# Relu and square of the boundary units: one VectorE instruction in place of two on ScalarE

## The chip, the cores and the metric

The program runs on one core of one Trainium2 chip. A core has five engines that work through their own instruction queues in order: TensorE (PE in the profile, with the weight loads apart as PEld), VectorE (DVE), ScalarE (ACT), GpSimd (POOL) and SyncE (SP, which only issues transfers here). They signal each other by semaphores. The metric is the device time of the whole program in microseconds (us).

## The reference

```
p_packed = sm_attn(p, k, v)                       # 32 packed rows per batch and head
out      = sm_attn(q, p_packed, p_packed)         # 8 batches x 576 tokens, 8 heads x 64
x = out as (4608 tokens, 512)
h = maximum(x @ w_in, 0);  x = (h * h) @ w_out    # 512 -> 2048 -> 512
logits = x @ w_gate + modality_bias[modality_id]  # 8 experts, the greatest is taken
out[tokens of e] = gate * (maximum(x @ w1[e], 0) @ w2[e])   # 512 -> 1024 -> 512
```

All inputs are float32. A float32 product is made on TensorE as three products of a high and a low part (hi x hi, hi x lo, lo x hi), and making those parts is most of the work of VectorE and ScalarE.

## The kernel before, in words

The 4608 tokens go through the middle layers in 12 **units** of 384 tokens (`UT` = 3 tiles of 128). For unit `u` the first layer is done in 16 **blocks** `f` of 128 hidden columns (`layer1`), each followed, one block later, by the second layer of the block before (`layer2`, 9 matmuls of 512 columns into the accumulators `acc`, L534). The packed values of a batch are multiplied with `w_in` ahead of time, so `layer1` multiplies attention weights (`a2T`) with a block that belongs to one batch (`ring`, `head`).

A batch has 576 tokens, so every third unit (1, 4, 7 and 10) holds tokens of two batches. The other eight units make a block by 12 matmuls (L508), and ScalarE reads the sum from PSUM for relu (L523, `r<-ph`). A **boundary unit** makes each of its two **halves** of 192 tokens by four matmuls (L514, L516 twice, L517) into two groups of columns of one bank; ScalarE copies one group to `r` (L520) and VectorE adds the other (L521). Then relu (L523, `r<-r`), square (L524) and the high part (L525, writes `ghl`) follow on ScalarE, and the low part (L527, `ghl<-r,ghl`) on VectorE. There are two buffers each of `r` and `ghl` and two PSUM banks `h`.

Beside this each unit carries background work, paced by counters in the loop over `f`: the attention of the next unit (`att2`), splitting the next batch's blocks (L426 on ScalarE, L427 on GpSimd), and, for the unit before, the copy of the accumulators to `rows` (`evacuate`, L545 on VectorE) and 24 multiplications with the gate's weights, one for each tile and expert (`tail`, L555). In units 4 and 10 `route` follows: it ranks the tokens by expert, with one-hot rows (`od`, `om`, L689 and L691), matmuls of them (`pl`, L699) and two additions to the list `lst` (L705). In unit 10 `tables` makes from `lst` the row numbers `idx_g` (L745), by which GpSimd gathers the rows of the first group of the expert layers (`xg`, L790); TensorE turns these (`tr`, L804), and the expert layers follow.

The order of instructions on each engine in this part is set by the framework's scheduler: it takes ready instructions by priority, and L520 to L527 stand 40 places ahead of their place in the program (`high_priority(offset=CHAIN)`). Once written, an engine's order is fixed.

Of the kernel before, what the change touches and what calls it, by code (L numbers as in the profile page):

```python
# [15 lines left out]
AF = mybir.ActivationFunctionType  # L16
ALU = mybir.AluOpType
# [9 lines left out]
def tile_pack_attention_moe_moe2(  # L27
# [15 lines left out]
    nc = tc.nc  # L43
# [211 lines left out]
    def bank(tag, name):  # L255
        if "early" in held:
            return held["early"].tile([P, 512], F32, tag="e", name=name, bufs=4)
        return held["ps" + tag].tile([P, 512], F32, tag=tag, name=name)
# [148 lines left out]
    def block(b, f):  # L407
        return (NF * b + f) % RING

    def blocks(i, n):  # L410
        t = held["head" if i < HEAD else "ring"]
        i -= 0 if i < HEAD else HEAD
        return t[:, i : i + n]
# [16 lines left out]
    def parts(t0, n):  # L430
        got, t = [], t0
        while t < t0 + n:
            b = t // S
            e = min(t0 + n, (b + 1) * S)
            got.append((b, t - t0, e - t))
            t = e
        return got
# [59 lines left out]
    def layer1(u, f):  # L497
        a = a2T[u]
        r = held["g"].tile([P, UW], F32, tag="r", name="r")
        hl = held["g"].tile([P, 2, UW], F32R, tag="ghl", name="ghl")  # L500
        ps = parts(u * UW, UW)
        if len(ps) == 1:
            ph = bank("h", "ph")[:, :UW]
            t = blocks(block(ps[0][0], f), 1)[:, 0]
            i = 0
            for c in range(NPC):
                for x, y in ((0, 0), (0, 1), (1, 0)):
                    nc.tensor.matmul(ph, t[:, x, c, :], a[:, y, c, :], start=(i == 0), stop=(i == 3 * NPC - 1))  # L508
                    i += 1
        for b, off, n in ps if len(ps) > 1 else ():  # L510
            ph = bank("h", "ph")[:, : 2 * n]
            both = ph.rearrange("p (y n) -> p y n", y=2)
            t = blocks(block(b, f), 1)[:, 0]
            nc.tensor.matmul(both, t[:, 0, 0, :], a[:, :, 0, off : off + n], start=True, stop=False)  # L514
            for c in range(NPC):
                nc.tensor.matmul(both[:, 0], t[:, 1, c, :], a[:, 0, c, off : off + n], start=False, stop=False)  # L516
            nc.tensor.matmul(both, t[:, 0, 1, :], a[:, :, 1, off : off + n], start=False, stop=True)  # L517
            with tc.high_priority(offset=CHAIN):
                rn = r[:, off : off + n]
                nc.scalar.activation(out=rn, in_=both[:, 1], func=AF.Copy)  # L520
                nc.vector.tensor_tensor(out=rn, in0=both[:, 0], in1=rn, op=ALU.add)  # L521
        with tc.high_priority(offset=CHAIN if u else 0):
            nc.scalar.activation(out=r, in_=ph if len(ps) == 1 else r, func=AF.Relu)  # L523
            nc.scalar.activation(out=r, in_=r, func=AF.Square)  # L524
            nc.scalar.activation(out=hl[:, 0], in_=r, func=AF.Copy)  # L525
            eng = nc.vector if u else nc.gpsimd
            eng.tensor_tensor(out=hl[:, 1], in0=r, in1=hl[:, 0].bitcast(F32), op=ALU.subtract)  # L527
        return hl
# [399 lines left out]
    with tc.manual_schedule():  # L928
# [90 lines left out]
        for f in range(NF):  # L1019
            if f:  # L1020
                load_out(f + 3)
            hl = layer1(0, f)
            pw_next("tt")
            if f > 3:
                pw_next("th")
            if f > 2:
                next(bg, None)
            put()
            if pend is not None:
                if f == 1:  # L1030
                    held["acc"] = [bank("acc", "acc") for _ in range(UT)]
                layer2(held["acc"], *pend)
            pend = (f, hl)
            if f:
                halve_out(f)
            if f == 0:
                compact(NQ - 1)
            if 0 < f < NU - 1:
                for _ in conv_out(f + 1):
                    pass  # L1040
            if f in (4, 7):
                for _ in conv_in(14 + f // 7):
                    pass
            if f + 2 < NF:
                split_pw(0, f + 2)
            ahead(0, 0, f)
# [29 lines left out]
    for u in range(1, NUN):  # L1076
        pair, k = divmod(u, UPP)
        last = u == NUN - 1
        if u == 1:
            st1.close()  # L1080
            nc.sync.dma_start(
                wgb.rearrange("p e d -> p (e d)"), w_gateT.rearrange("e d -> (e d)").partition_broadcast(P)
            )
            held["xg"] = ctx.enter_context(tc.tile_pool(name="xg", bufs=2, side="right"))
        bga = Paced([] if last else [att2(u + 1)], R_ATT)
        for f in range(NF):
            hl = layer1(u, f)
            if pend is not None:
                second_layer()
            pend = (u, f, hl)  # L1090
            if f == 0:
                gens, n = background(u)
                bgt = Paced(gens, n / ((NF - 6 if last else NF) - 1.5))
            bga.step()
            bgt.step()
            ahead(pair, k, f)
            if last and f == NF - 6:
                bgt.finish()
                bgt = Paced([weights1(0)], 1)
        bga.finish()  # L1100
        bgt.finish()
# [80 lines left out]
```

## Time and profile before

| | before |
|---|---|
| median of 3 runs | 1226.17 us (1223.72 to 1228.62) |
| the profiled execution's own time | 1226.34 us |
| its span, first to last instruction | 1224.5 us |
| PE busy | 1186.8 us (97%) |
| DVE busy | 810.2 us (66%) |
| ACT busy | 625.6 us (51%) |
| POOL busy | 278.0 us (23%) |

Busy times count an instruction from its start to its end. On DVE and ACT the next instruction may start before the end of the last one, so a row of back-to-back instructions advances by less than the sum of their lengths.

### The profile page before, as it was taken

The numbers are of one execution on the slowest core, as the hardware profiler recorded it, in microseconds if no ns is written. First come the engines' busy times: TensorE is split into PE (matmuls) and PEld (weight loads), VectorE is DVE, ScalarE is ACT, GpSimd is POOL, SyncE is SP. The second block draws the span as 40 slices with busy tenths as digits, with TensorE's granted clock in tenths as the row PEclk, the third lists the DMA queues.
The fourth block names the chain that finished last, engine by engine and source line by source line (L and its number), as shares of the span: only waits on it lengthen the run. The fifth ranks groups of instructions, "written<-read, shape, count | busy, mean of one in ns | idle before, by whom it ended". The sixth has DMA issues, their size and how long they took to land.

```text
span 1224.5 us, 17896 instructions
## 1 busy us (share of the span) xinstructions
PE 1186.8 (97%) x6036; PEld 976.1 (80%) x6036; DVE 810.2 (66%) x2123; ACT 625.6 (51%) x1332; POOL 278.0 (23%) x347
## 2 busy tenths in 40 slices
PE   6999999999999999999999999999999999999995
PEld 4776568888888888888888887888888888888884
DVE  4777989597669857695975797889445345345331
ACT  5667777755467664567554676524233333333220
POOL 2316563221022320032210222003112122123001
PEclk9999999999999999999999999999999999999998
DMA  9999883220112220122101113307254254254211
GB/s 327 365 335 312 268 268 103 87 72 27 44 44 80 61 70 9 48 67 87 61 27 44 44 68 100 130 7 245 80 180 156 75 185 156 69 191 151 71 56 37
DMA packets 76086, 147.13 MB, mean 120 GB/s; under 512 B 7504, under 2 KB 27088, under 8 KB 75856
## 3 DMA queue, kind: packets, MB, share of 16 engines
q1 hardware_dynamic: 70224, 126.72, 31.3%
q0 software_dynamic: 5760, 19.17, 4.8%
q8 instruction: 49, 0.80, 0.3%
q14 instruction: 53, 0.43, 0.1%
HBM read 109.92 MB, written 33.85 MB: 117 GB/s over the span
## 4 chain that ended last, share of the span: by engine, by line
PE 76%; DMA 11%; DVE 8%; issue 2%; ACT 1%; POOL 1%; SPq 1%; POOLq 0%; DVEq 0%; ACTq 0%
PE acc L534 26%; PE h L828 17%; PE o L855 16%; PE ph L508 10%; DMA early<-in_v 4%; DVE rows L555 3%; DMA pw_d<-pws 2%; PE s L456 2%; PE tr L804 1%; PE ph L516 1%; PE ph L517 1%; PE ph L514 1%; DMA wgb<-in_k 1%; DVE r L521 1%; DMA rows<-in_k 1%
## 5 line engine op out<-in xcount | busy, mean ns | idle before, releaser
L534 PE MATMUL acc<-wb,ghl 128*128 128x512 f32 x1728 | 442.5, 399 | 1.9 <-ACT ghl L525 1.6
L534 PEld LDWEIGHTS acc<-wb,ghl 128*128 128x128 f32 x1728 | 317.9, 189 | 68.8 <-ACT ghl L525 6.4
L555 DVE SCALAR_TENSOR_TENSOR rows<-rows,wgb 128x512 f32<-128x512 f32 x288 | 212.1, 736 | 4.5 <-DMA wgb<-in_moe_w_gate 0.9
L828 PE MATMUL h<-xt,wb 128*128 128x512 f32 x864 | 213.1, 397 | 0.0
L828 PEld LDWEIGHTS h<-xt,wb 128*128 128x128 f32 x864 | 161.7, 188 | 38.5
L527 DVE TENSOR_TENSOR ghl<-r,ghl 128x384 fp32r<-128x384 f32 x176 | 106.8, 608 | 77.0 <-ACT ghl L525 76.9
L525 ACT ACTIVATE ghl<-r 128x384 fp32r<-128x384 f32 x192 | 100.0, 522 | 81.6 <-PE acc L534 79.2
L840 DVE SCALAR_TENSOR_TENSOR ht<-h,ht 128x512 fp32r<-128x512 f32 x72 | 49.3, 688 | 114.1 <-ACT ht L840 114.1
L840 ACT ACTIVATE ht<-h 128x512 fp32r<-128x512 f32 x72 | 42.7, 592 | 144.2 <-PE h L828 141.1
L866 POOL DMA_INDIRECT out<-wgb,idx_s x36 | 37.4, 1040 | 336.1 <-DVE wgb L864 251.4
L855 PE MATMUL o<-head,ht 128*128 128x512 f32 x432 | 111.8, 395 | 0.2 <-DVE wgb L864 0.2
L855 PE MATMUL o<-ring,ht 128*128 128x512 f32 x432 | 111.8, 395 | 0.0
L524 ACT ACTIVATE r<-r 128x384 f32<-128x384 f32 x192 | 99.9, 523 | 4.4
L855 PEld LDWEIGHTS o<-head,ht 128*128 128x128 f32 x432 | 80.4, 188 | 18.6 <-DVE wgb L864 0.6
L855 PEld LDWEIGHTS o<-ring,ht 128*128 128x128 f32 x432 | 80.4, 188 | 16.7
L427 POOL TENSOR_TENSOR ring<-praw,ring 128x256 fp32r<-128x256 f32 x70 | 58.8, 840 | 153.4 <-ACT ring L426 125.3
L523 ACT ACTIVATE r<-ph 128x384 f32<-128x384 f32 x128 | 62.0, 485 | 61.6 <-PE ph L508 33.8
L508 PE MATMUL ph<-a2T,ring 128*128 128x384 f32 x420 | 85.1, 339 | 0.0
L508 PEld LDWEIGHTS ph<-a2T,ring 128*128 128x128 f32 x420 | 74.7, 188 | 4.6
L508 PE MATMUL ph<-a2T,head 128*128 128x384 f32 x348 | 72.1, 341 | 1.1 <-ACT head L426 0.9
L761 DVE TENSOR_TENSOR wb<-wraw,wb 128x1024 fp32r<-128x1024 f32 x36 | 44.0, 1224 | 43.4 <-ACT wb L760 42.8
L427 POOL TENSOR_TENSOR head<-praw,head 128x256 fp32r<-128x256 f32 x50 | 43.2, 864 | 113.2 <-ACT head L426 113.0
(208 smaller groups left out, 1649.4 us busy)
## 6 DMA issues: line engine op xcount, KB each, us to landing
wraw<-in_moe_w SPq DMA_DIRECT2D x72, 512.0 KB, 3.5
praw<-pw_d SPq DMA_DIRECT2D x112, 128.0 KB, 2.6
x_d<-rows SPq DMA_DIRECT2D x12, 792.0 KB, 3.8
qT<-in_q SPq DMA_DIRECT2D x36, 256.0 KB, 2.9
early<-in_v SPq DMA_DIRECT2D x16, 512.0 KB, 7.8
pw_d<-pws SPq DMA_DIRECT2D x16, 512.0 KB, 5.9
stage<-in_moe_w_in SPq DMA_DIRECT2D x14, 512.0 KB, 9.1
pw_d<-pws SPq DMA_DIRECT2D x16, 384.0 KB, 4.7
```

The costliest lines, as they stand in the source:

```text
L427: nc.gpsimd.tensor_tensor(out=t[:, 1], in0=raw, in1=t[:, 0].bitcast(F32), op=ALU.subtract)
L508: nc.tensor.matmul(ph, t[:, x, c, :], a[:, y, c, :], start=(i == 0), stop=(i == 3 * NPC - 1))
L523: nc.scalar.activation(out=r, in_=ph if len(ps) == 1 else r, func=AF.Relu)
L524: nc.scalar.activation(out=r, in_=r, func=AF.Square)
L525: nc.scalar.activation(out=hl[:, 0], in_=r, func=AF.Copy)
L527: eng.tensor_tensor(out=hl[:, 1], in0=r, in1=hl[:, 0].bitcast(F32), op=ALU.subtract)
L534: nc.tensor.matmul(acc[t], hl[:, x, t * P : (t + 1) * P], w_out_block(f)[:, y, :], start=(f == 0 and x == 0 and y == 0), stop=(f == NF - 1 ...
L555: nc.vector.scalar_tensor_tensor(out=junk, in0=row[:, t, :DM], scalar=1.0, in1=wgb[:, e], op0=ALU.mult, op1=ALU.mult, accum_out=one)
L761: nc.vector.tensor_tensor(out=t[:, 1, :], in0=raw, in1=t[:, 0, :].bitcast(F32), op=ALU.subtract)
L828: nc.tensor.matmul(ph, half1(g, c)[:, x, f * P : (f + 1) * P], xs[c][:, y, :], start=(i == 0), stop=(i == 3 * NDC - 1),)
L840: done = nc.scalar.activation(out=h[:, 0, :], in_=ph, func=AF.Relu), nc.vector.scalar_tensor_tensor(out=h[:, 1, :], in0=ph, scalar=0.0, in ...
L855: nc.tensor.matmul(po, hs[f][:, x, t * P : (t + 1) * P], second(f)[:, y, :], start=(i == 0), stop=(i == 3 * NFE - 1),)
```

## The change: what it does

In a boundary unit the two ScalarE instructions L523 and L524 are replaced by one VectorE instruction that computes max(r, 0) * r, from `r` and `r` in SBUF, in place. There are 4 x 16 such blocks: 64 relu and 64 square instructions of 128x384 leave ScalarE and 64 SCALAR_TENSOR_TENSOR of 128x384 come to VectorE. The other units are as they were.

```diff
         with tc.high_priority(offset=CHAIN if u else 0):
-            nc.scalar.activation(out=r, in_=ph if len(ps) == 1 else r, func=AF.Relu)
-            nc.scalar.activation(out=r, in_=r, func=AF.Square)
+            if len(ps) == 1:
+                nc.scalar.activation(out=r, in_=ph, func=AF.Relu)
+                nc.scalar.activation(out=r, in_=r, func=AF.Square)
+            else:
+                nc.vector.scalar_tensor_tensor(out=r, in0=r, scalar=0.0, in1=r, op0=ALU.max, op1=ALU.mult)
             nc.scalar.activation(out=hl[:, 0], in_=r, func=AF.Copy)
             eng = nc.vector if u else nc.gpsimd
             eng.tensor_tensor(out=hl[:, 1], in0=r, in1=hl[:, 0].bitcast(F32), op=ALU.subtract)
```

The changed file is three lines longer: the new instruction is L527 there, and the old L525, L527, L534, L545, L555, L699, L705 and L804 are L528, L530, L537, L548, L558, L702, L708 and L807.

The scheduler also writes another order. This is VectorE in the middle of unit 10, among the logit multiplications; `r<-ph,r` is the addition of a half, `ghl<-r,ghl` the low part of a block. Before:

```order
L555 SCALAR_TENSOR_TENSOR rows,lg_all<-rows,wgb 128x512 x3
L527 TENSOR_TENSOR ghl<-r,ghl 128x384
L521 TENSOR_TENSOR r<-ph,r 128x192
L555 SCALAR_TENSOR_TENSOR rows,lg_all<-rows,wgb 128x512
L521 TENSOR_TENSOR r<-ph,r 128x192
L555 SCALAR_TENSOR_TENSOR rows,lg_all<-rows,wgb 128x512 x3
L527 TENSOR_TENSOR ghl<-r,ghl 128x384
```

The changed kernel at the same place:

```order
L530 TENSOR_TENSOR ghl<-r,ghl 128x384
L521 TENSOR_TENSOR r<-ph,r 128x192
L558 SCALAR_TENSOR_TENSOR rows,lg_all<-rows,wgb 128x512
L527 SCALAR_TENSOR_TENSOR r<-r 128x384
L558 SCALAR_TENSOR_TENSOR rows,lg_all<-rows,wgb 128x512
L521 TENSOR_TENSOR r<-ph,r 128x192
L530 TENSOR_TENSOR ghl<-r,ghl 128x384
```

A block now has one instruction more on VectorE, and fewer logit multiplications stand between two low parts.

The second place is TensorE at the end of unit 10, from the matmuls of the routing (`pl`) to the first turned rows of the gather (`tr`). Before:

```order
L699 MATMUL pl<-od,om 128x184
L534 MATMUL acc<-wb_1710,ghl 128x512 x3
L514 MATMUL ph<-a2T,head 128x384
L516 MATMUL ph<-a2T,head 128x192 x2
L517 MATMUL ph<-a2T,head 128x384
L514 MATMUL ph<-a2T,head 128x384
L516 MATMUL ph<-a2T,head 128x192 x2
L517 MATMUL ph<-a2T,head 128x384
L534 MATMUL acc<-wb_1710,ghl 128x512 x9
L514 MATMUL ph<-a2T,head 128x384
L516 MATMUL ph<-a2T,head 128x192 x2
L517 MATMUL ph<-a2T,head 128x384
```

After these rows stand, before, one `tr` matmul, nine more of `acc`, five `tr`, and six more of `acc`. In the changed kernel:

```order
L702 MATMUL pl<-od,om 128x184
L537 MATMUL acc<-wb_1802,ghl 128x512 x12
L807 MATMUL tr<-ident,xg 128x128 x3
L487 MATMUL ta_7664<-ident,e 128x128 x2
L807 MATMUL tr<-ident,xg 128x128 x5
L508 MATMUL ph<-a2T,head 128x384 x2
```

The last `pl` moved behind all the first-layer matmuls of unit 10, and 12 matmuls of `acc` are left between it and the first `tr`.

The third place is VectorE just behind that, where `idx_g` is made in the changed kernel:

```order
L708 TENSOR_TENSOR lst<-pl,lst 128x92
L527 SCALAR_TENSOR_TENSOR r<-r 128x384
L469 TENSOR_TENSOR e<-s_7531,mx 128x256
L708 TENSOR_TENSOR lst<-pl,lst 128x92
L745 TENSOR_SCALAR s_7559<-lst 128x28
L749 SCALAR_TENSOR_TENSOR s_7560<-lst,slot 128x28
L530 TENSOR_TENSOR ghl<-r,ghl 128x384
L748 CAST idx_g<-s_7559 128x28
```

Here a relu-and-square has come in between the two additions to `lst`, and a low part stands ahead of `idx_g`.

Counted in the two orders, VectorE holds from the copy of the accumulators that opens a unit's logits to the 24th logit multiplication (the **front** of the unit):

| front of unit | halves L521 | new instruction | low parts | logits | others |
|---|---|---|---|---|---|
| 1, before / after | 16 / 20 | 0 / 9 | 9 / 9 | 24 / 24 | 20 / 23 |
| 4, before / after | 16 / 18 | 0 / 8 | 8 / 8 | 24 / 24 | 12 / 12 |
| 7, before / after | 15 / 18 | 0 / 9 | 6 / 8 | 24 / 24 | 21 / 22 |
| 10, before / after | 14 / 16 | 0 / 8 | 7 / 7 | 24 / 24 | 6 / 6 |
| 10, to the second addition to `lst` | 26 / 30 | 0 / 15 | 13 / 14 | 24 / 24 | 82 / 82 |

## Rows read from the trace of the kernel before

**Rows 1.** Windows: start:end, length, busy time (instructions) of each engine, clock, DMA
```profile
core 0: us, PE busy (x) PEld busy (x) DVE busy (x) ACT busy (x) POOL busy (x), PEclk, DMA share, GB/s
184.40:221.00 36.60, 36.09 (x203) 30.98 (x202) 34.90 (x104) 25.54 (x66) 11.30 (x14) 1.00 0.33 98
350.90:381.00 30.10, 29.54 (x160) 25.46 (x160) 29.85 (x86) 21.85 (x55) 9.34 (x10) 1.00 0.20 59
381.00:402.00 21.00, 21.00 (x128) 17.86 (x127) 19.76 (x88) 15.11 (x38) 4.74 (x7) 1.00 0.28 95
516.80:547.00 30.20, 28.87 (x163) 24.80 (x162) 30.08 (x90) 20.08 (x54) 10.35 (x12) 1.00 0.22 65
547.00:571.20 24.20, 24.20 (x136) 21.33 (x136) 14.24 (x41) 17.39 (x44) 7.72 (x11) 1.00 0.31 99
684.40:713.70 29.30, 28.11 (x147) 23.85 (x146) 28.91 (x92) 20.60 (x53) 7.73 (x9) 1.00 0.13 37
713.70:735.00 21.30, 21.30 (x125) 18.32 (x124) 19.22 (x90) 15.02 (x37) 5.32 (x6) 1.00 0.27 101
```

**Rows 2.** Timeline of TensorE in unit 4: start, length, operation, [idle before, releaser]
```profile
352.54 2.26 PE L534 MATMUL acc<-wb,ghl 128*128 128x512 f32 x9
...
355.78 2.25 PE L534 MATMUL acc<-wb,ghl 128*128 128x512 f32 x9
...
375.88 0.44 PE L514 MATMUL ph<-a2T,head 128*128 128x384 f32 x1 [0.30 <-DVE r L521]
...
377.55 0.73 PE L534 MATMUL acc<-wb,ghl 128*128 128x512 f32 x2 [0.26 <-ACT ghl L525]
```

**Rows 3.** Groups by line and shape: busy, mean ns of one, idle before
```profile
L555 DVE SCALAR_TENSOR_TENSOR rows<-rows,wgb 128x512 f32<-128x512 f32 x288 | 212.1, 736 | 4.5 <-DMA wgb<-in_moe_w_gate 0.9
...
L527 DVE TENSOR_TENSOR ghl<-r,ghl 128x384 fp32r<-128x384 f32 x176 | 106.8, 608 | 77.0 <-ACT ghl L525 76.9
...
L524 ACT ACTIVATE r<-r 128x384 f32<-128x384 f32 x192 | 99.9, 523 | 4.4
...
L523 ACT ACTIVATE r<-r 128x384 f32<-128x384 f32 x64 | 33.3, 521 | 17.8 <-DVE r L521 17.7
```

**Rows 4.** Timeline of VectorE in unit 4
```profile
370.61 0.56 DVE L527 TENSOR_TENSOR ghl<-r,ghl 128x384 fp32r<-128x384 f32 x1
371.08 0.35 DVE L521 TENSOR_TENSOR r<-ph,r 128x192 f32<-128x192 f32 x1
...
372.24 0.35 DVE L521 TENSOR_TENSOR r<-ph,r 128x192 f32<-128x192 f32 x1
372.51 0.68 DVE L555 SCALAR_TENSOR_TENSOR rows<-rows,wgb 128x512 f32<-128x512 f32 x1
373.12 0.07 DVE L555 DVE_READ_ACCUMULATOR rows<-rows,wgb 128x1 f32 x1
```

**Rows 5.** Line 527: ns of one, least/median/greatest, first and last start
```profile
L527 DVE TENSOR_TENSOR ghl<-r,ghl x176: 501/557/1093, 185.1 to 793.8; 128x384 fp32r<-128x384 f32 x176
```

**Rows 6.** Timeline of VectorE at the start of unit 10's logits
```profile
684.48 0.69 DVE L545 COPY rows<-acc 128x512 f32<-128x512 f32 x1 [1.36 <-PE acc L534]
```

**Rows 7.** Chain that ended last, end of unit 10: start, time on the chain, what
```profile
730.84 0.27 DVE lst L705
...
736.27 5.70 DMA xg<-x_d,idx_g
...
742.02 0.44 PE tr L804 x2
```

**Rows 8.** Timeline of TensorE from the last `pl` to the `tr` matmuls
```profile
730.11 0.41 PE L699 MATMUL pl<-od,om 128*128 128x184 f16 x3
...
735.74 0.33 PE L804 MATMUL tr<-ident,xg 128*128 128x128 f32 x1 [0.68 <-DMA xg<-x_d,idx_g]
...
738.63 0.33 PE L804 MATMUL tr<-ident,xg 128*128 128x128 f32 x1 [0.36 <-DMA xg<-x_d,idx_g]
...
742.02 0.44 PE L804 MATMUL tr<-ident,xg 128*128 128x128 f32 x2 [1.12 <-DMA xg<-x_d,idx_g]
```

## The prediction

> **What bounds the kernel now.** I read the windows first, cut at the boundary units: from where VectorE copies the accumulators until the logits are through, and the rest of the unit [rows 1]. In the fronts of units 4, 7 and 10 TensorE is busy 29.54 of 30.10 us, 28.87 of 30.20 and 28.11 of 29.30, and VectorE 29.85, 30.08 and 28.91. Both are full, so the bound there is whichever falls behind. ScalarE is busy some 70% (21.85 of 30.10). In unit 1 VectorE has 1.7 us left in 36.6. In the second parts the picture splits: in unit 7 VectorE is busy 14.24 of 24.20, but in units 4 and 10, where the routing stands, 19.76 of 21.00 and 19.22 of 21.30.
>
> The timeline of TensorE in unit 4 says who is behind. A block takes 355.78 - 352.54 = 3.24 us while all goes well; near the end of the front the first layer waits for a half's addition on VectorE and then the second layer for the high part [rows 2]. The high part was late because its chain began late, at an addition that stood behind logit multiplications in VectorE's queue. So in the fronts VectorE sets the pace, by a little: TensorE's idle time in the four windows is 0.51 + 0.56 + 1.33 + 1.19 = 3.6 us.
>
> The chain that ended last shows one more place [rows 7]. At the end of unit 10 it runs from VectorE's second addition to `lst` (done at 730.84 + 0.27 = 731.11), through `idx_g` and four gathers on GpSimd, to the last rows landing and the `tr` matmuls at 742.02: 10.9 us that nothing shortens. TensorE waits three times in it, 0.68, 0.36 and 1.12 us [rows 8], although most of it was covered by matmuls of unit 10. From there the expert layers start, so a microsecond later in `lst` is one later at the end, as long as the cover doesn't grow.
>
> **What the change removes.** In each of the 64 blocks ScalarE loses 521 + 523 ns [rows 3], 67 us in all. ScalarE is not the bound in any of these windows, so this time itself is worth nothing. What may be worth something is that the way from the second half's addition to the high part gets shorter. I set that to nothing, since it was the wait in VectorE's queue ahead of that way which held TensorE; the limit on the gain is the 3.6 us of idle time, taken up as a rival below.
>
> **What it adds, and its price.** The trace has no relu-and-square on VectorE. The nearest row is the low part, L527: two inputs in SBUF, the same 384 elements. Back to back it advances the queue by 371.08 - 370.61 = 0.47 us [rows 4]; its median of 557 ns is longer since the next instruction starts some 0.08 us before its end, and its mean is 608 [rows 3, 5], which with the same overlap gives 0.53. I take 0.50. Bounds: 0.42 (the least length, 501 ns, less the overlap) and 0.61, the advance of a logit multiplication (373.12 - 372.51), which is the same operation with 512 elements. A half's addition advances the queue by 372.51 - 372.24 = 0.27.
>
> The Trainium skill ("Perfetto Trace Analysis", Optimizing Scalar/DVE Operations) advises moving work from VectorE to ScalarE where VectorE is saturated; this change goes the other way. If all 64 new instructions counted in full, as that rule read strictly would have it, the sum would be 64 x 0.50 = 32 us slower; by the windows only part of them fall where VectorE is full, and I count those alone.
>
> **Unit by unit.** The changed order spreads the 24 logit multiplications over more blocks, so the front holds more work, but TensorE also gets more done in it. For each front: the added VectorE work less 3.24 us for each block (two halves) that TensorE does more.
>
> Unit 4: eight new instructions and two additions, 8 x 0.50 + 2 x 0.27 = 4.5, less one block: 1.3 us. Unit 7: 9 x 0.50 + 3 x 0.27 + 2 low parts x 0.47 = 6.25, less one and a half blocks, 4.86: 1.4 us. Unit 1: 9 x 0.50 + 4 x 0.27 = 5.6 (with three small ones some 6), less two blocks, 6.5: nothing. Behind the fronts unit 1 and unit 7 have VectorE time to spare (10 us in unit 7 [rows 1]), which covers the rest of the new instructions; were that cover gone, the seven left in unit 7 would cost 3.5. In unit 4 the rest of the routing can run into unit 5, where nothing gathers by it.
>
> Unit 10 is where the list must be ready. From the copy at 684.48 [rows 6] to the end of the second addition at 731.11 VectorE needs 46.6 us, and it is busy for all but some 2 of them [rows 1]. The changed order holds 15 new instructions, four half additions and one low part more up to the same point: 15 x 0.50 + 4 x 0.27 + 0.47 = 9.1 us. The matmuls of the last `pl` have moved behind all first-layer matmuls of the unit, and 12 matmuls of `acc` (12 x 2.25 / 9 = 3.0 us by [rows 2]) are left as cover for the 10.9 us, where 27 of `acc` and three halves were. What was cover now lies ahead of `pl`, so when the rows land TensorE has done about the same work as before, and the expert layers start later by the whole 9.1. Queued behind the `tr` matmuls on TensorE is all of unit 11, which can't step in.
>
> The sum is 0 + 1.3 + 1.4 + 9.1 = 11.8 us on the profiled execution's 1226.34, 1238.1; the median of the runs is 0.2 lower, so I say 1238. With 32 new instructions in the sum (8, 9 and 15), the price bounds shift it by -2.6 and +3.5; if unit 10 fills its idle 2 us, by -2. That gives 1233.5 to 1241.6 for this case.
>
> **Rivals.** First, the list is not the bound: the changed order asks VectorE for the routing later, because TensorE's work before it is longer, and the 10.9 us stay covered. Then unit 10 costs only its front, 8 x 0.50 + 2 x 0.27 - 3.24 = 1.3, and the whole is 1226.3 + 4.0 = 1230.3. For it speaks that TensorE, too, comes later to `pl` in the new order; against it that VectorE had about 2 us idle where 9 are added, and that less cover, not more, stands behind `pl`. It needs 7.8 of the 9.1 hidden.
>
> Second, on the other side: TensorE's waits in the fronts come from the length of the way over ScalarE, not from VectorE's queue. The way gets shorter by 521 + 523 less some 500 ns in each block, and the idle 3.6 us go: 1226.3 - 3.6 = 1222.7. For it speaks that one of the two waits in rows 2 is for ScalarE's high part; against it VectorE's 98 to 99%. It decides if the front of unit 4 gets shorter than 30.1 us for the same blocks.
>
> Third, worse: the new instruction meets GpSimd. The low part's longest is 1093 ns against a median of 557 [rows 5], and most of GpSimd's busy time, 9.34 us in the front of unit 4 [rows 1], is tensor work on SBUF. If half of the 32 are lengthened by 0.53 us, 8.5 us come on top: 1246.6. The Trainium skill ("SBUF — State Buffer", Who interferes with whom) says that a VectorE instruction with two inputs in SBUF and a GpSimd instruction that reads SBUF exclude each other, the later one waiting to the end. By that rule the trace agrees, since the longest is the median and one GpSimd instruction's remainder; my 0.53 in the price holds the usual share of such cases already.
>
> That the change does nothing can't be: the order shows 64 instructions moved.
>
> **How the numbers follow.** Less than 0.5% (6.1 us) is about what a measurement of this kernel can't tell from no change: 1220.0 to 1232.3. The forecast gets 0.57, the first rival 0.20, the second 0.10, the third 0.13. Slower by over 0.5% are the forecast and the third, with a little of the first: 0.72. The second lies within 0.5% in the main, with a tail past 1220 where the waits' restarts go as well: faster 0.05. The rest, 0.23, is the same. The range leaves out most of the second rival and the upper half of the third: 1226 to 1244; the forecast's own is 1233.5 to 1241.6.
>
> **What would show it.** In the trace of the changed kernel: 64 instructions of 128x384 on VectorE's new line with a median near 0.56 us; VectorE at 98% or more in the fronts of units 4, 7 and 10; from the copy that opens unit 10's logits to the second `lst` addition some 56 us in place of 46.6; TensorE's waits for the gather and for `pl` together some 10 us in place of 2.2 (the 9.1 less the front's 1.3, added to them). Units 2, 5 and 8 should be as long as before. The prediction is wrong if the new instruction runs well under 0.42 or over 0.61 us, if `lst` is late but TensorE's waits before `tr` don't grow, or if the way over ScalarE was what counted and the fronts shrink.

## The result, and the profile after

The changed kernel takes 1241.1 us, the median of six runs (1238.97 to 1244.12), beside 1226.22 us for the kernel before on the same chip (six runs). The ratio is 1.0136, with a 95% interval of 1.0116 to 1.0155: the change makes the kernel slower. The prediction said 1238 with a range of 1226 to 1244.

The profiled execution of the changed kernel took 1239.04 us, its span is 1237.2 us. The first part of its page gives busy time, share of the span and instructions of each engine:

```profile
PE 1194.5 (97%) x6036; PEld 978.1 (79%) x6036; DVE 842.1 (68%) x2187; ACT 562.9 (45%) x1204; POOL 276.9 (22%) x347
```

VectorE rose by 31.9 us to 842.1, ScalarE fell by 62.7 to 562.9. The time went up by about half of what VectorE gained; whether anything came back for what ScalarE lost is tested below.

**Where the time went.** Like a ruler along the program, the start of the first `acc` matmul of each unit (L534, now L537) was read from TensorE's timeline in both traces. These are the differences between such starts, in us:

| from the first `acc` of unit | before | after | change | predicted |
|---|---|---|---|---|
| 0 to 2 (unit 1) | 147.59 | 148.67 | +1.1 | 0 |
| 2 to 3 | 51.54 | 51.52 | 0 | 0 |
| 3 to 5 (unit 4) | 114.86 | 116.15 | +1.3 | +1.3 |
| 5 to 6 | 53.02 | 53.55 | +0.5 | 0 |
| 6 to 8 (unit 7) | 114.15 | 117.24 | +3.1 | +1.4 |
| 8 to 9 | 51.54 | 51.52 | 0 | 0 |
| 9 to 11 (unit 10) | 116.07 | 125.72 | +9.65 | +9.1 |
| sum | 648.77 | 664.37 | +15.6 | +11.8 |

The sum agrees with the medians, 1241.1 - 1226.2 = 14.9 us. (The profiled execution itself reached unit 0 some 2.9 us sooner than the one before, so the two spans differ by 12.7 only; that lies ahead of unit 0's first `acc`.)

The marks themselves move a little against the other matmuls, since TensorE's order changed too, and this shifts time between rows. From 5 to 6 TensorE has 275 matmuls in place of 265: ten of the attention (eight `s`, two `ta`) that it has fewer from 3 to 5. So units 4 and 5 belong together, and lose 1.8 us. From 1 to 2 it has six first-layer matmuls fewer, some 1.05 us, and from 9 to 11 six more. And 0.7 of unit 1's 1.1 lie ahead of its own first `acc`, in a stretch (0 to 1) that took from 85.96 to 88.39 us in six of the traces, with and without the change. From 1 to 2 the loss is 0.3 us, or some 1.4 for the same matmuls.

From the first `acc` of unit 1 to that of unit 11 as a whole, before and then in the changed kernel:

```profile
core 0: us, PE busy (x) PEld busy (x) DVE busy (x) ACT busy (x) POOL busy (x), PEclk, DMA share, GB/s
186.52:748.24 561.72, 555.97 (x2945) 479.65 (x2945) 423.75 (x1331) 340.45 (x806) 120.52 (x147) 1.00 0.18 56
184.32:760.90 576.58, 563.72 (x2944) 481.80 (x2944) 459.18 (x1410) 278.79 (x680) 122.35 (x147) 0.99 0.18 55
```

Of the 14.9 us, TensorE's idle time is 7.1 (12.86 in place of 5.75). The other 7.8 are busy time, with the same matmuls but one record. Some 2.4 of them are a lower clock at the end of unit 10 (below). The remaining 5 come with the changed order of the matmuls, or with waits too short to show between records that overlap; no run separates the two.

**The fronts.** These are windows of the changed kernel, in the columns of [rows 1]: the front of units 1, 4, 7 and 10, now with the new instructions in it.

```profile
182.90:222.30 39.40, 38.55 (x212) 32.64 (x212) 38.79 (x111) 16.74 (x48) 11.38 (x13) 1.00 0.30 84
...
350.50:385.00 34.50, 32.90 (x176) 27.93 (x174) 34.47 (x100) 14.47 (x43) 9.82 (x12) 1.00 0.22 62
...
518.60:556.00 37.40, 34.24 (x187) 29.26 (x186) 37.40 (x105) 14.97 (x45) 11.37 (x13) 1.00 0.23 62
...
689.00:721.00 32.00, 30.99 (x157) 25.65 (x157) 32.00 (x92) 13.64 (x38) 10.22 (x10) 1.00 0.12 35
```

In the fronts of units 4, 7 and 10 VectorE is busy 34.47 of 34.50, 37.40 of 37.40 and 32.00 of 32.00 us: it has next to no gap now, and TensorE's idle time there is 1.60, 3.16 and 1.01 us in place of 0.56, 1.33 and 1.19 [rows 1]. A front is longer (34.5 against 30.1 in unit 4) and holds more blocks, so its length alone isn't the loss; the table by units is.

**The new instruction.** The view by source line gives least, median and greatest length in ns:

```profile
L527 DVE SCALAR_TENSOR_TENSOR r<-r x64: 498/550/1102, 180.6 to 743.3; 128x384 f32<-128x384 f32 x64
```

It costs what the low part costs [rows 5]. Its mean is 616; from the start of one to the start of the next instruction the 64 advance VectorE's queue by 0.47 us in the median and 0.54 in the mean (of the 57 with another instruction right behind), where 0.50 was taken. Ten of the 64 are longer than 1.15 times the median, 4.3 us in all, and four of these ten stand in the front of unit 7.

**Unit 7** lost more than was predicted. These are all of TensorE's waits in its front, from the timeline; the time in brackets is idle time before the matmul:

```profile
527.78 1.65 PE L537 MATMUL acc<-wb,ghl 128*128 128x512 f32 x6 [0.36 <-ACT ghl L528]
532.58 0.45 PE L514 MATMUL ph<-a2T,ring 128*128 128x384 f32 x1 [1.32 <-DVE r L521]
544.34 1.67 PE L537 MATMUL acc<-wb,ghl 128*128 128x512 f32 x6 [0.54 <-ACT ghl L528]
549.20 1.67 PE L537 MATMUL acc<-wb,ghl 128*128 128x512 f32 x6 [0.24 <-ACT ghl L528]
553.50 0.74 PE L537 MATMUL acc<-wb,ghl 128*128 128x512 f32 x2 [0.69 <-ACT ghl L528]
```

They sum to 3.15 us. The longest ends when a half's addition is done, and VectorE's timeline shows what stood ahead of that addition:

```profile
530.51 0.68 DVE L558 SCALAR_TENSOR_TENSOR rows<-rows,wgb 128x512 f32<-128x512 f32 x1
...
531.12 1.07 DVE L527 SCALAR_TENSOR_TENSOR r<-r 128x384 f32<-128x384 f32 x1
532.18 0.35 DVE L521 TENSOR_TENSOR r<-ph,r 128x192 f32<-128x192 f32 x1
...
534.89 1.07 DVE L527 SCALAR_TENSOR_TENSOR r<-r 128x384 f32<-128x384 f32 x1
...
538.78 0.92 DVE L527 SCALAR_TENSOR_TENSOR r<-r 128x384 f32<-128x384 f32 x1
...
547.51 1.08 DVE L527 SCALAR_TENSOR_TENSOR r<-r 128x384 f32<-128x384 f32 x1
```

The new instruction took 1.07 us there, 0.52 over its median. Three more of the nine in this front were lengthened, by 0.52, 0.37 and 0.53 us, and together the nine advance VectorE's queue by 6.1 us. GpSimd's timeline has a tensor instruction with two SBUF inputs beside the first of them, from 530.75 to 531.77:

```profile
530.75 1.02 POOL L427 TENSOR_TENSOR ring<-praw,ring 128x256 fp32r<-128x256 f32 x1 [2.99 <-ACT ring L426]
```

The Trainium skill ("SBUF — State Buffer", Who interferes with whom) says that such a pair excludes each other. The row agrees: from the end of the GpSimd instruction to that of the new one are 0.42 us, near the 0.47 by which an undisturbed one advances the queue. Each of the other three has a GpSimd tensor instruction beside it too, which began first.

**Unit 10** was read in three stretches: to VectorE's copy that opens the logits (688.96), to the end of the second addition to `lst` (744.36), and to the first `acc` of unit 11. The windows of the changed kernel:

```profile
635.18:688.96 53.78, 53.78 (x276) 45.86 (x276) 32.53 (x96) 25.35 (x57) 3.63 (x5) 1.00 0.11 35
688.96:744.36 55.40, 53.25 (x282) 44.06 (x280) 54.76 (x190) 22.18 (x64) 13.23 (x14) 1.00 0.11 36
744.36:760.90 16.54, 11.88 (x55) 10.22 (x56) 13.47 (x41) 6.89 (x16) 7.54 (x11) 0.79 0.40 127
```

The same three of the kernel before, which the rows ahead of the prediction don't hold:

```profile
632.17:684.50 52.33, 52.33 (x273) 45.24 (x273) 31.42 (x94) 25.76 (x59) 4.56 (x6) 1.00 0.10 33
684.50:731.10 46.60, 45.41 (x249) 38.79 (x248) 45.55 (x169) 33.29 (x84) 10.76 (x13) 1.00 0.14 45
731.10:748.24 17.14, 14.98 (x87) 12.77 (x86) 9.40 (x30) 10.35 (x23) 7.15 (x11) 1.00 0.35 114
```

From the copy to the list it is 55.4 us in place of 46.6, with VectorE busy all but 0.6: 8.8 more, where 9.1 were predicted. The first stretch gives 1.45 more, with TensorE busy throughout; it holds six whole first-layer matmuls more (79 L508 in place of 73) and three small ones of a half fewer, which is about half of it. The last stretch does not fit the prediction. It has 55 matmuls of TensorE in place of 87, since the others now stand ahead of the list, and yet it is only 0.6 us shorter. TensorE's timeline says why:

```profile
744.47 2.36 PE L537 MATMUL acc<-wb,ghl 128*128 128x512 f32 x9 [0.73 <-ACT ghl L528]
...
749.32 0.33 PE L807 MATMUL tr<-ident,xg 128*128 128x128 f32 x1 [2.50 <-DMA xg<-x_d,idx_g]
750.73 0.47 PE L807 MATMUL tr<-ident,xg 128*128 128x128 f32 x1 [1.08 <-DMA xg<-x_d,idx_g]
752.18 0.47 PE L807 MATMUL tr<-ident,xg 128*128 128x128 f32 x1 [0.98 <-DMA xg<-x_d,idx_g]
...
753.95 0.99 PE L508 MATMUL ph<-a2T,head 128*128 128x384 f32 x2
754.74 1.05 PE L807 MATMUL tr<-ident,xg 128*128 128x128 f32 x4
755.45 2.88 PE L508 MATMUL ph<-a2T,head 128*128 128x384 f32 x10
758.17 0.60 PE L807 MATMUL tr<-ident,xg 128*128 128x128 f32 x4
...
758.71 2.36 PE L508 MATMUL ph<-a2T,head 128*128 128x384 f32 x12
760.90 0.62 PE L537 MATMUL acc<-wb,ghl 128*128 128x512 f32 x2
```

The waits for the gather are 2.50 + 1.08 + 0.98 = 4.56 us, against 0.68 + 0.36 + 1.12 = 2.16 [rows 8]. After them TensorE ran slower for a while: the first twelve L508 advanced it by (754.74 - 753.95) + (758.17 - 755.45) = 3.51 us, the next twelve by 760.90 - 758.71 = 2.19. The same 23 matmuls (L487 x2, L807 x9, L508 x12) from 752.45 to 758.17 advanced it by 5.72 us, and in the kernel before by 3.29 when the waits and the `acc` matmuls between them are left out: 2.4 us more. The granted clock (third from the end of a row) in windows of the same stretch:

```profile
746.00:749.00 3.00, 0.82 (x4) 0.34 (x2) 2.39 (x7) 1.09 (x2) 2.40 (x3) 1.00 0.78 238
749.00:752.00 3.00, 0.80 (x2) 0.32 (x2) 2.90 (x7) 0.00 (x0) 2.67 (x4) 0.76 0.68 189
752.00:754.00 2.00, 1.82 (x9) 1.53 (x9) 0.61 (x4) 0.38 (x1) 0.61 (x4) 0.50 0.36 112
754.00:756.00 2.00, 2.00 (x10) 1.90 (x9) 1.81 (x6) 1.25 (x3) 0.00 (x0) 0.50 0.00 0
756.00:758.00 2.00, 2.00 (x10) 2.00 (x9) 2.00 (x7) 0.92 (x2) 0.00 (x0) 0.65 0.00 0
758.00:760.00 2.00, 2.00 (x17) 1.95 (x17) 1.28 (x5) 1.99 (x5) 0.80 (x1) 1.00 0.00 0
```

It fell to 0.50, that is to 1.2 of 2.4 GHz, while TensorE waited for the gather (busy 0.82 and 0.80 us in the first two windows), and came back between 756 and 758. In the kernel before it is 1.00 in every window from 728 to 752.

### The profile page after: what moved, and what is told of

Read it like the earlier page. It is cut to its first block, busy times and chain, and to the rows that moved or that the text cites. A ratio compares the mean times of both kernels' runs of the same rounds, so it can differ in the third digit from the quotient of the medians.

```text
span 1237.2 us, 17838 instructions
## 1 busy us (share of the span) xinstructions
PE 1194.5 (97%) x6036; PEld 978.1 (79%) x6036; DVE 842.1 (68%) x2187; ACT 562.9 (45%) x1204; POOL 276.9 (22%) x347
## 4 chain that ended last, share of the span: by engine, by line
PE 73%; DVE 16%; DMA 6%; issue 2%; ACT 1%; SPq 0%; POOL 0%; POOLq 0%; DVEq 0%; ACTq 0%
PE acc L537 23%; PE h L831 16%; PE o L858 16%; PE ph L508 10%; DVE rows L558 5%; DMA pw_d<-pws 2%; DVE r L527 2%; DVE r L521 2%; PE s L456 1%; PE tr L807 1%; DMA early<-in_v 1%; DVE ghl L530 1%; PE pq L351 1%; DVE tf L218 1%; DVE tf L217 1%
## 5 line engine op out<-in xcount | busy, mean ns | idle before, releaser
L537 PE MATMUL acc<-wb,ghl 128*128 128x512 f32 x1728 | 444.4, 399 | 5.6 <-ACT ghl L528 4.9
L537 PEld LDWEIGHTS acc<-wb,ghl 128*128 128x128 f32 x1728 | 317.1, 188 | 76.0 <-ACT ghl L528 11.9
L558 DVE SCALAR_TENSOR_TENSOR rows<-rows,wgb 128x512 f32<-128x512 f32 x288 | 215.2, 747 | 3.8 <-DMA wgb<-in_moe_w_gate 0.5
L528 ACT ACTIVATE ghl<-r 128x384 fp32r<-128x384 f32 x192 | 100.6, 524 | 148.1 <-PE acc L537 91.7
L530 DVE TENSOR_TENSOR ghl<-r,ghl 128x384 fp32r<-128x384 f32 x176 | 103.1, 586 | 61.7 <-ACT ghl L528 61.5
L427 POOL TENSOR_TENSOR ring<-praw,ring 128x256 fp32r<-128x256 f32 x70 | 61.8, 884 | 149.5 <-ACT ring L426 137.2
L508 PE MATMUL ph<-a2T,ring 128*128 128x384 f32 x420 | 85.0, 340 | 0.0
L524 ACT ACTIVATE r<-ph 128x384 f32<-128x384 f32 x128 | 61.5, 482 | 44.2 <-PE ph L508 40.8
L508 PEld LDWEIGHTS ph<-a2T,ring 128*128 128x128 f32 x420 | 74.1, 188 | 4.1
L508 PE MATMUL ph<-a2T,head 128*128 128x384 f32 x348 | 74.0, 348 | 0.0
L520 ACT ACTIVATE r<-ph 128x192 f32<-128x192 f32 x128 | 41.6, 326 | 69.8 <-PE ph L517 65.5
L525 ACT ACTIVATE r<-r 128x384 f32<-128x384 f32 x128 | 66.9, 524 | 3.2
```

Source lines behind the costliest of these rows:

```text
L427: nc.gpsimd.tensor_tensor(out=t[:, 1], in0=raw, in1=t[:, 0].bitcast(F32), op=ALU.subtract)
L524: nc.scalar.activation(out=r, in_=ph, func=AF.Relu)
L537: nc.tensor.matmul(acc[t], hl[:, x, t * P : (t + 1) * P], w_out_block(f)[:, y, :], start=(f == 0 and x == 0 and y == 0), stop=(f == NF - 1 ...
L558: nc.vector.scalar_tensor_tensor(out=junk, in0=row[:, t, :DM], scalar=1.0, in1=wgb[:, e], op0=ALU.mult, op1=ALU.mult, accum_out=one)
```

## The experiments

Each ratio is to the kernel before, run on the same chip, with its 95% interval.

**Only unit 10, and only units 1, 4 and 7.** The theory of the prediction prices the two places apart: 9.1 us where the list must be ready, 2.7 in the other fronts. One run has the change in unit 10 alone (its edit to the changed kernel):

```diff
-            if len(ps) == 1:
-                nc.scalar.activation(out=r, in_=ph, func=AF.Relu)
+            if u != 10:
+                nc.scalar.activation(out=r, in_=ph if len(ps) == 1 else r, func=AF.Relu)
                 nc.scalar.activation(out=r, in_=r, func=AF.Square)
```

> Relu and square on VectorE in unit 10 alone, units 1, 4 and 7 as before. If the time goes where VectorE's queue makes the list of unit 10 late and the gather behind it uncovered: 8 to 10 us slower than before, with the copy-to-list stretch of unit 10 near 55 us. If the cost is a little in every boundary block (a longer hand-off from engine to engine): a quarter of the 14.9 us, some 4.

Measured: 1235.06 us, 1.0081 (1.0058 to 1.0104), 9.9 us slower, as expected. The fronts of units 4 and 7 are as before: in the windows of [rows 1] TensorE is busy 29.53 of 30.10 and 28.90 of 30.20 us. VectorE's timeline gives the way to the list:

```profile
684.24 0.69 DVE L548 COPY rows<-acc 128x512 f32<-128x512 f32 x1 [0.19 <-PE acc L537]
...
739.10 0.24 DVE L708 TENSOR_TENSOR lst<-pl,lst 128x92 f32<-128x92 f32 x1
```

That is 739.34 - 684.24 = 55.1 us, as in the full change, and TensorE then waits for the gather:

```profile
746.01 0.48 PE L807 MATMUL tr<-ident,xg 128*128 128x128 f32 x1 [4.80 <-DMA xg<-x_d,idx_g]
```

By the ruler this trace loses 7.3 us from 9 to 11 (123.39 in place of 116.07) and nothing in units 4, 5 and 7.

The other run has `if u not in (1, 4, 7)` in the same place.

> Relu and square on VectorE in units 1, 4 and 7, unit 10 as before. By VectorE's full queue: the fronts of units 4 and 7 pay 1 to 3 us each, unit 1 next to nothing, together 3 to 6 us slower than before, and the stretch from the copy to the list in unit 10 stays near 46.6 us. By an equal cost in every boundary block: 11 us slower.

Measured: 1233.26 us, 1.0070 (1.0043 to 1.0096), 8.6 us by the ratio, more than the 3 to 6 expected. Its trace repeats the steps of the full change in units 4, 5 and 7 (+1.3, +0.5 and +3.1), and from copy to list it needs 48.3 us. From 9 to 11 it loses 2.7 us (118.81), although unit 10 is as before: 1.3 ahead of the copy that opens the logits and 1.6 from there to the list, the six matmuls of the shifted mark among them. So unit 10's own instructions are some 7.3 of the 9.65 us lost there; unit 7's 3.1 are its own and no echo of unit 10.

**An instruction that nobody reads.** Is it VectorE's time, or that the values now pass through another engine? The kernel before, with one more instruction of the same operation and shape in each boundary block, which reads a constant and writes a spare buffer; ScalarE keeps relu and square.

```diff
         with tc.high_priority(offset=CHAIN if u else 0):
+            if len(ps) > 1:
+                same = ident.unsqueeze(1).to_broadcast([P, UT, P])
+                spare = junk[:, :UW].rearrange("p (t x) -> p t x", t=UT)
+                nc.vector.scalar_tensor_tensor(out=spare, in0=same, scalar=0.0, in1=same, op0=ALU.max, op1=ALU.mult)
             nc.scalar.activation(out=r, in_=ph if len(ps) == 1 else r, func=AF.Relu)
```

> The kernel before, relu and square on ScalarE, and in each boundary block one more VectorE instruction of the same operation and shape (128x384, two inputs in SBUF) on constant data, whose result nobody reads; so the way from the sum to the high part is as before, and only VectorE's time is taken. If that time is the cause: 10 to 15 us slower than before, like the change. If the cause is the way itself, now over VectorE in place of ScalarE: within 3 us of before.

Measured: 1242.46 us, 1.0136 (1.0110 to 1.0163), the loss of the change itself. (By the ratio that is 16.7 us, a little over the 10 to 15 expected.) The added line by source, and the wait for the gather in TensorE's timeline:

```profile
L526 DVE SCALAR_TENSOR_TENSOR rows<-ident x64: 540/548/1172, 123.2 to 731.4; 128x384 f32<-128x384 f32 x64
```

```profile
752.68 0.47 PE L808 MATMUL tr<-ident,xg 128*128 128x128 f32 x1 [8.54 <-DMA xg<-x_d,idx_g]
```

It isn't the same loss in every place: from 1 to 2 it is 4.6 us and from 9 to 11 12.0, but units 4 and 5 together lose only 0.5 and unit 7 0.6. The scheduler could put the free-standing instruction elsewhere. So some 0.5 us of VectorE's queue in each block is enough to lose 16 us, most of it at the list, with the way from the sum to the high part as before. That VectorE's time alone makes the loss of units 4 and 7 is not shown by this run. And with ScalarE's work kept the loss is the same: the 67 us taken from ScalarE were worth nothing that shows.

**The square alone on VectorE.** If the hand-over between the engines counted, keeping relu on ScalarE should change something (the edit is to the changed kernel):

```diff
-                nc.vector.scalar_tensor_tensor(out=r, in0=r, scalar=0.0, in1=r, op0=ALU.max, op1=ALU.mult)
+                nc.scalar.activation(out=r, in_=r, func=AF.Relu)
+                nc.vector.tensor_tensor(out=r, in0=r, in1=r, op=ALU.mult)
```

> The changed kernel with relu back on ScalarE and only the square on VectorE (r * r, 128x384, two inputs in SBUF). VectorE's time is the same as in the change, some 0.5 us a block. If that time is the cause: 12 to 17 us slower than before, as the change. If the two instructions saved on ScalarE are worth anything, or the hand-offs cost: slower than the change by some 64 x 0.5 us where the way decides, 20 us or more slower than before.

Measured: 1243.18 us, 1.0140 (1.0105 to 1.0175): no difference from the change that shows. The multiplication has a median of 555 ns, like the new instruction. One ScalarE instruction and one hand-over more in each block cost nothing that stands out of an interval of 4 us to either side; the 20 us or more of the other reading lie at its upper end.

**VectorE relieved.** The opposite test takes work from VectorE. The halves are summed by TensorE (six matmuls of 192 columns each into one group, twice), so that the copy L520 and the addition L521 fall away and relu reads PSUM as in the other units.

```diff
+        ph = bank("h", "ph")[:, :UW]
+        for b, off, n in ps:
+            t = blocks(block(b, f), 1)[:, 0]
             i = 0
             for c in range(NPC):
                 for x, y in ((0, 0), (0, 1), (1, 0)):
-                    nc.tensor.matmul(ph, t[:, x, c, :], a[:, y, c, :], start=(i == 0), stop=(i == 3 * NPC - 1))
+                    nc.tensor.matmul(
+                        ph[:, off : off + n], t[:, x, c, :], a[:, y, c, off : off + n],
+                        start=(i == 0), stop=(i == 3 * NPC - 1),
+                    )
...
-        for b, off, n in ps if len(ps) > 1 else ():
...
```

> The kernel before, but a half of a boundary block is summed on TensorE by six matmuls of 192 columns, as many columns as the four before, so VectorE's additions (32 x 0.27 = 8.6 us a unit) and ScalarE's copies go, and relu reads PSUM. If VectorE's queue is the bound in the boundary units: faster than before by 3 to 8 us, TensorE's waits in the fronts gone, less up to 4 us for two more weight loads in each half. If VectorE's queue is not the bound: slower by those up to 4 us.

Measured: 1227.59 us, 1.0022 (1.0007 to 1.0038), no gain, where 3 to 8 us were expected. The price on TensorE had been put at up to 4 us, which no run shows. Its timeline in unit 4:

```profile
361.37 2.30 PE L525 MATMUL acc<-wb,ghl 128*128 128x512 f32 x9
...
364.04 0.83 PE L508 MATMUL ph<-a2T,head 128*128 128x192 f32 x6
...
365.26 2.28 PE L525 MATMUL acc<-wb,ghl 128*128 128x512 f32 x9
```

One such matmul follows the next after 0.111 us, so a block's twelve take 1.33 us where the eight of before took 1.15: 64 x 0.185 = 11.8 us more on TensorE, for a loss of 2.7. So the relief of VectorE and of ScalarE's copies was worth some 9 us; that is a difference of two numbers, not a measurement of its own. To keep the price down, the same was done in blocks 1 to 9 only (`one = len(ps) == 1 or 0 < f < 10`), where the fronts lie:

> The kernel before, with the six matmuls of 192 columns only in blocks 1 to 9 of a boundary unit, where the logits stand on VectorE, and the four matmuls with VectorE's addition in the others. In the trace of the kernel with six matmuls in all blocks a matmul of 192 columns follows the next after 0.111 us, so a block takes 1.33 us in place of 1.15: 36 blocks cost 6.6 us where 64 cost 11.8, and that kernel was only some 2.7 us slower than before, so the relief of VectorE gave some 9 us. If all of that comes in the fronts: 1 to 3 us faster than before. If it comes from the end of unit 10: 3 to 6 us slower.

Measured: 1227.28 us, 1.0024 (1.0008 to 1.0040), 2.9 us slower at a price of 36 x 0.185 = 6.7: a relief of some 3.7, about the 3.6 us by which TensorE idles in the fronts of before [rows 1]. The gain of 1 to 3 us that was expected for this case didn't come. What the other blocks of six matmuls gained, some 5 us, isn't located.

**The list a unit earlier.** If the wait at the end of unit 10 is the list, it should go when that list is ready early. Here it covers the first 24 tiles of 128 tokens in place of 28, and row numbers for 6 groups in place of 7 are made from it; so list, `tables` and the first gather come about the end of unit 8 and not of unit 10. One line does it, in the kernel before and in the changed one:

```diff
-    J_A = NTL - 2 * NTT
+    J_A = NTL - 3 * NTT
```

> The kernel before with the first list taken over 24 tokens' tiles in place of 28 (J_A = NTL - 3 * NTT), so that the routing's list, the tables and the first gather fall into unit 8, which has one batch, and no longer to the end of unit 10. By the theory that unit 10 ends on a chain from VectorE to the gather: the 2.2 us of waits before the turned rows go, and unit 10's second part is lighter on VectorE; 2 to 4 us faster than before. If the gather's chain does not matter: no change, or a little slower by one more small routing pass.

> The changed kernel with the same earlier list. If most of the change's loss is the late list of unit 10 with the gather uncovered behind it: 8 to 11 us faster than the changed kernel, so 3 to 6 us slower than the kernel before, what the fronts of units 1, 4, 7 and 10 cost. If the loss is the VectorE time or the longer way in every block, wherever the list stands: still some 12 us slower than before.

Measured: 1223.21 us, 0.9989 (0.9975 to 1.0003), without the change, and 1229.56, 1.0047 (1.0031 to 1.0063), with it. In both the `tr` matmuls wait for nothing; this is the changed one:

```profile
638.39 0.49 PE L807 MATMUL tr<-ident,xg 128*128 128x128 f32 x3
```

With the list out of the way the change costs 1229.56 - 1223.21 = 6.4 us in place of some 15 to 17. The ruler shows where the rest went: from 9 to 11 it is 116.54 us with the change and 116.08 without, so unit 10 loses 0.5 us in place of 9.65, while units 4, 5 and 7 lose the same as ever (+1.3, +0.5, +3.1); the six matmuls of the shifted mark, 1.0 us, come from 8 to 9 here. So some 8 to 10 us of the loss were the list. TensorE's granted clock stays at 1.00 there from 735 to 760. The kernel before gains nearly nothing by the same edit, where 2 to 4 us were expected, though the 2.2 us of waits for the gather are gone.

**The logits spread.** The fronts are full because 24 logit multiplications are let loose at once. With the early list there is no hurry for them, so on top of it, in blocks 0 to 11 of boundary units, a block's step of the logits and the routing is held until that block's low part is issued:

```diff
-            eng.tensor_tensor(out=hl[:, 1], in0=r, in1=hl[:, 0].bitcast(F32), op=ALU.subtract)
+            held["low"] = eng.tensor_tensor(out=hl[:, 1], in0=r, in1=hl[:, 0].bitcast(F32), op=ALU.subtract)
...
-            bgt.step()
+            with ExitStack() as behind:
+                if k == 1 and f < NF - 4:
+                    behind.enter_context(tc.issue_after(held["low"].ins))
+                bgt.step()
```

> The kernel before with the earlier list, and in boundary units a step of the logits and the routing is held until the low part of the block at hand is done, up to block 11, so VectorE takes some two logits a block where it took three or four. If VectorE's full queue in the fronts is what TensorE waits for: the fronts' waits shrink, and the kernel is 2 to 6 us faster than before. If the waits come from the way over ScalarE: as fast as the kernel with the earlier list alone, within 1 us.

The second run has the same edits in the changed kernel:

> The same with relu and square as one VectorE instruction in boundary units. With two logits a block VectorE has some 0.5 us a block to spare in units 1 and 7, so there the new instruction should cost next to nothing; in unit 4 the routing still follows. By the theory of VectorE's queue: within 4 us of the kernel with the logits spread and ScalarE's relu and square, and no more than 2 us slower than before. If the longer way or the hand-offs cost: 5 us or more slower than that kernel.

The third is spread, but the copy of the second accumulator that stands in boundary units (that of the unit before) is made by ScalarE in place of VectorE:

```diff
-            if t == 1:
+            if t == 1 and u % 3:
                 nc.vector.tensor_copy(row[:, t, :DM], acc[t])
...
```

> The kernel with the logits spread, and in boundary units ScalarE makes the copy of the second accumulator (592 ns) that VectorE made (690 ns). One instruction less on VectorE in each of four units: 0 to 2 us faster than with the logits spread alone if VectorE still decides there, the same if it doesn't.

Measured: spread 1219.05 us, 0.9950 (0.9930 to 0.9970); with the change on top 1222.89, 0.9980 (0.9967 to 0.9992); with the second accumulator copied by ScalarE as well 1219.74, 0.9957 (0.9941 to 0.9972). Windows of spread over the whole of units 4, 7 and 10, since the logits now reach over it:

```profile
346.00:398.00 52.00, 51.14 (x287) 43.96 (x286) 49.40 (x169) 37.99 (x95) 13.78 (x17) 1.00 0.23 72
512.00:565.00 53.00, 52.58 (x293) 46.10 (x292) 42.74 (x127) 38.06 (x99) 15.40 (x20) 1.00 0.23 66
679.00:732.00 53.00, 52.15 (x286) 45.08 (x285) 47.51 (x164) 38.04 (x94) 14.02 (x16) 1.00 0.19 61
```

VectorE has 2.6, 10.3 and 5.5 us to spare, where front and rest of these units together had 1.5, 10.1 and 2.5 before [rows 1]: in unit 7 the reserve is no greater, but VectorE is now 74 to 84% busy in each quarter of the window, where it was full in the front and 59% busy behind it. From the first `acc` of unit 0 to that of unit 11 it is 643.80 us, 5.0 less than before. From unit 1's to unit 11's, as above for the other two kernels:

```profile
184.74:741.13 556.39, 554.27 (x2953) 480.63 (x2952) 430.65 (x1366) 341.72 (x809) 124.14 (x153) 1.00 0.19 59
```

TensorE's idle time is 2.1 us there in place of 5.75, 3.6 of the 5.3 us gained; the rest is busy time and not located. In the kernel with the earlier list alone it is 3.7 us. In spread_after, the window of unit 7:

```profile
516.00:569.00 53.00, 52.74 (x292) 45.98 (x292) 49.16 (x137) 24.67 (x68) 16.18 (x20) 1.00 0.24 66
```

VectorE takes 6.4 us more for the added instructions and still has room, but over the program the change costs 3.8 us even here. So spreading takes away most of the loss, not all; TensorE's idle time from unit 1 to 11 is 3.2 us in place of 2.1, and the rest isn't located. Spread is the fastest version tried; that ScalarE copies one more accumulator adds nothing to it.

## Why the prediction was right

**The price** held: 0.50 was taken, 0.54 is the mean advance, 0.47 the median. With 32 instructions in the sum the difference is 1.3 us. The rest of the step, that a new instruction costs only where VectorE is full, held in the main: all 64 in full would have been 32 us, and half of that came. The Trainium skill ("Perfetto Trace Analysis", Optimizing Scalar/DVE Operations) says that moving work from a saturated VectorE to ScalarE may make sense. It gives no price, so the 32 us were the prediction's own strict reading; the direction agrees with this kernel, where the move the other way cost 14.9 us.

**Unit 4** came as predicted, +1.3, if its own row is taken, and so did the full VectorE in the three fronts. But ten attention matmuls moved from its row into unit 5's, which was said to be as long as before and lost 0.5; the two together lost 1.8. **Unit 1** was put at nothing and lost 0.3 us between its own marks, some 1.4 with the six matmuls that moved out of them; VectorE's reserve of 1.7 us there [rows 1] did not hold all nine.

**Unit 7** is the term that was mis-sized: 3.1 in place of 1.4. The nine new instructions stood in it with 4.5 us, on the argument that the mean price holds the usual share of lengthened ones. They advanced VectorE by 6.1, since four of the nine were lengthened beside GpSimd, by 1.9 us together, where the program has ten among 64. The 1.6 us more are about the missing 1.7. On TensorE the 3.1 are 1.8 us of waits (3.15 for 1.33) and 1.3 of busy time with the same matmuls. That the lengthening makes the loss is read from rows; logit multiplications in this front were lengthened too, no run took GpSimd's work away, and the idle instruction lost only 0.6 us here, so the cause stays open.

**Unit 10** was right in its sum (9.65 for 9.1) and in its first half (copy to list 55.4 us, 55.7 predicted). That the sum is so near is in part luck: 2.7 of it come in unit 10 when only the other units are changed, and with unit 10 alone changed it loses 7.3. Inside the second half two errors cancel. The way from the list to the last rows, taken as fixed at 10.9 us, was 752.18 - 744.36 = 7.8; the gather's part on the chain fell from 5.70 [rows 7] to 3.85 us, and why was not tried. And TensorE's waits, said to become some 10 us, were 4.6. What stood in their place: 32 fewer matmuls lay behind the list, some 5.5 us by the mean of before (14.98 / 87), and the loss came as waits (2.4 more) and as matmuls at the lower clock (5.72 us for 3.29, 2.4 more). The step "the expert layers start later by the whole 9.1" was right; the sign by which it was to be seen was not.

**The rivals.** The first, that the list isn't the bound, fell: unit 10 alone loses 9.9 us, and with the list early unit 10 loses 0.5 and the change 6.4 in place of some 15. The second, that the shorter way over VectorE gains the idle 3.6 us, fell: the waits in the fronts grew, to 5.8 us in units 4, 7 and 10. That it is VectorE's time and not the other way is shown for the list, where an instruction that touches no value of that way loses as much, but for units 4 and 7 it is argued. No run adds the instructions and keeps the order of before, so what the added time costs and what the scheduler's new order costs are not told apart. The third, GpSimd, is there in part: 10 of 64 were lengthened, not half, by 4.3 us in all, of which 1.9 in unit 7. Its reading of the low part's longest was a little off: in the kernel before it ended 0.41 us after the GpSimd instruction beside it, not a median of 0.56.

## What to carry to other kernels

Before an instruction moves to another engine, cut that engine's time by stages: here VectorE is busy 66% overall and about 99% in the fronts of units 4, 7 and 10, and there the added time showed: eight or nine instructions of half a microsecond cost 1.8 us in units 4 and 5 and 3.1 in unit 7. Look also for the one result that a later stage waits for; here a queue 8.8 us longer ahead of it cost 9.65 us in that unit, though VectorE had room afterwards, and 0.5 once the result was made earlier. The gain lay the other way: bring that result forward and spread the background work over the busy stretch (1219.05 us, 0.995 of before; the first alone gave 0.9989, no gain clear of noise).

## What was not expected of the hardware

TensorE's granted clock halved in the wait for the gather or at its end. In the change TensorE waited 2.50, 1.08 and 0.98 us with single matmuls between; the clock was 0.50 at 752 and full again by 758, at a cost of some 2.4 us in matmuls. The same is in three other traces: with unit 10 alone, in the wait of 4.80 us, 0.50 to 0.52 from 744 to 751; with the idle instruction, in that of 8.54 us, about 0.50 from 748 to 761; with the square alone, after that of 4.33 us, 0.50 from 758 to 762. With waits of 0.68, 0.36 and 1.12 us, in the kernel before, it stayed at 1.00. The Trainium skill ("TensorE: Matmul & The Clock Gate", HAM oscillation — how this bites in real kernels) tells of matmuls that restart at half clock after a wait for a transfer; these traces agree. So these waits cost more than their length: in the change 2.4 us on top of 4.6.
